# Two more products with the identity turned into DMA transposes, in an attention and mixer kernel on one core

## The chip, the cores and the metric

The kernel runs on one core of one Trainium2 chip, as one program. Its time is the device time of one execution in microseconds (us); of several executions the median is taken. Lines such as L384 are line numbers of the kernel before.

The core's engines run their own instruction queues side by side: TensorE (PE in the profile) does matmuls and writes PSUM; VectorE (DVE) and ScalarE (ACT) work element by element; GpSimd (POOL) here mostly issues loads that convert float32 to float16; SyncE (SP) issues stores and DMA transposes. All DMAs are carried out by 16 DMA engines.

## The reference

There are 8 batches, 8 heads, 576 tokens, 16 beacon tokens and a head size of 64. First comes attention, causal over the tokens, with the beacons visible to all; then a mixer over the 512 channels of the 8 heads.

```python
k_all = np.concatenate([beacon_k, k], axis=2)
v_all = np.concatenate([beacon_v, v], axis=2)
scores = np.matmul(q, k_all.transpose(0, 1, 3, 2)) / np.sqrt(D)    # causal over the tokens
a = softmax(scores)
x = np.matmul(a, v_all)                                            # as (batch, token, channel)
h = x.transpose(0, 2, 1) @ U @ V                                   # low rank (32) over the tokens
u = x + h.transpose(0, 2, 1)
out = u + np.maximum(u @ w_ch1, 0.0) @ w_ch2                       # 512 -> 2048 -> 512
```

## The kernel before

**Attention.** The heads are taken in pairs: pair `p` is batch `p // 4`, heads `2 * (p % 4)` and the next. For each pair the kernel needs q and k with the head size on the partitions (`qT`, `kT`), the scores (`score_units`, L329, the exponential on ACT in L335, the mask on DVE in L305 and L307), and the product with v (`av_unit`, L357). Its result, divided by the sum, goes to `xb` (L366), which holds x of one batch with tokens on the partitions.

For batches 0 to 3, q and k are turned on TensorE: the loads land in a staging tile, DVE copies a pair of heads into a packed tile `pr` (`regroup`, L252, and L254 for the beacons' rows of k), TensorE transposes it (L259), and DVE copies the result to `qT` and `kT` (L292, L297). For batches 4 to 7 (`DT0 = 4`), ten DMA transposes per batch do that from SP's queue (`turns`, L607). They are issued five at a time, in the order k0, q0, k1, q1, k2, then q2, k3, q3, k4, q4.

**Mixer.** `uT` holds u of all batches with the channels on the partitions. `mix_units` makes it for one batch: `head` (L393) is the product with U, `most` the product with V for the first 496 tokens (L417), `end` that for the last 80 (L429). Where `turned` is false, x itself is added inside the same PSUM banks by products with the identity (`x_into`, L372), and DVE and ACT copy the sum out (L406, L408). Where `turned` is true, `turn` has SP issue five DMA transposes of `xb` into `uT` (L384), and DVE adds the product to what they wrote (L404). Before the change, batch 0 has a version of its own (`first_mix`), batches 1 and 2 add x on TensorE, and batches 3 to 7 use the DMA transposes.

The two large products work on nine blocks of 512 rows of u, from `mlp_units`: 16 units `g_unit` (w_ch1, L487, with the ReLU on ACT in L500 or on DVE in L502), then four row tiles of four units `c_unit` each (w_ch2, L512). At the end u itself is added. For blocks 1 to 8, four DMA transposes (L481) have brought a piece of `uT` back to rows (`ut`), and DVE adds it while it copies the result out of PSUM (L525). For block 0, `turned` is false: four products with the identity add u in PSUM (L520), and DVE (L529) and ACT (L527) copy the result out in turns. Then SP stores it (L530).

**Order.** The order of the instructions of PE, ACT, DVE, SP and POOL is written out by hand. The units of the mixer stand in a list `queue`. After each step of a pair, `fill` takes some of them and puts them behind it, so that TensorE has large products to do while the pair's small steps wait for DVE and ACT. `feed` appends the units of a block as soon as its rows are known. `mix(b)` sets `head`, `most` and `end` of batch b into the list: `n` units stand ahead of `head`, `k` between `head` and `most`, three between `most` and `end`. In the loop over the pairs from batch 2 on, the step of pair 12 (batch 3, first pair) issues five of the fifth batch's ten transposes and then calls `mix(2)`; the step of pair 13 issues the other five. Scores of pair `p + 1` are computed at the start of the step of pair `p`, so the fifth batch's `qT` and `kT` are first read at the start of the step of pair 15.

Nothing reorders SP's queue: an instruction that waits holds up everything behind it. The same is true of DVE's.

Of the kernel before, what the change touches and what calls it, by code (L numbers as in the profile page):

```python
# [18 lines left out]
P = 128  # L19
# [11 lines left out]
def kernel(  # L31
# [14 lines left out]
    B, H, S, D = q.shape  # L46
# [6 lines left out]
    NH2 = H // 2  # L53
# [48 lines left out]
    def pst(shape, dtype, name):  # L102
        return psum.tile(shape, dtype, tag="ps", name=name)
# [364 lines left out]

        return head, begin, rest

    def mlp_units(t0, n, dst, flip, turned=True, last=False):


        units = []
        gT = {}
        held = {}

        def turn():
            ut = utp.tile([P, 4, DM], F16, name="ut", tag="ut")
            for cc in range(NCC):  # L480
                nc.sync.dma_start_transpose(out=ut[:, :, ts(cc, P)], in_=uT[:, cc, ds(t0, 4 * P)])  # L481
            gT["u"] = ut

        def g_part(dc, upto):
            g, done = held.get(dc) or (pst([P, 512], F32, name="gps"), 0)
            for cc in range(done, upto):
                nc.tensor.matmul(  # L487
                    g[:, 0:n], w1[:, cc, ts(dc, P)], uT[:, cc, ds(t0, n)], start=(cc == 0), stop=(cc == NCC - 1)
                )
            held[dc] = g, upto  # L490

        def g_unit(dc):
            if dc == 0:
                gT["t"] = gtp.tile([P, NDC, 512], F16, name="gT", tag="gT")
                if turned:
                    turn()
            g_part(dc, NCC)
            g, _ = held.pop(dc)
            if (dc % 3 if not turned else (dc + flip) % 2 or dc in (5, 6, 7)):
                nc.scalar.activation(out=gT["t"][:, dc, 0:n], in_=g[:, 0:n], func=AF.Relu)  # L500
            else:
                nc.vector.tensor_scalar_max(out=gT["t"][:, dc, 0:n], in0=g[:, 0:n], scalar1=0.0)  # L502

        cps = {}

        def c_unit(i, part):
            m = min(P, n - P * i)
            if part == 0:
                cps["t"] = pst([P, DM], F32, name="cps")
            ps = cps["t"]  # L510
            for dc in range(4 * part, 4 * part + 4):
                nc.tensor.matmul(  # L512
                    ps[:m, :], gT["t"][:, dc, ds(P * i, m)], w2[:, dc, :], start=(dc == 0),
                    stop=turned and dc == NDC - 1, skip_group_check=True,
                )
            if part == 3:
                ob = outp.tile([P, DM], F32, name="ob", tag="ob")
                if not turned:
                    for cc in range(NCC):
                        nc.tensor.matmul(  # L520
                            ps[:m, ts(cc, P)], uT[:, cc, ds(t0 + P * i, m)], ident, start=False, stop=True,
                            skip_group_check=True,
                        )
                if turned:
                    nc.vector.tensor_tensor(out=ob[:m, :], in0=ps[:m, :], in1=gT["u"][:m, i, :], op=ALU.add)  # L525
                elif i % 2:
                    nc.scalar.activation(out=ob[:m, :], in_=ps[:m, :], func=AF.Copy)  # L527
                else:
                    nc.vector.tensor_copy(out=ob[:m, :], in_=ps[:m, :])  # L529
                nc.sync.dma_start(out=dst(i, m), in_=ob[:m, :])  # L530

        def c_half(i, part):
            hs = ds(DM // 2 * (part // 2), DM // 2)
            if part % 2 == 0:
                cps["t"] = pst([P, DM // 2], F32, name="cph")
            for dc in range(NDC // 2 * (part % 2), NDC // 2 * (part % 2 + 1)):
                nc.tensor.matmul(  # L537
                    cps["t"], gT["t"][:, dc, ts(i, P)], w2[:, dc, hs], start=(dc == 0), stop=(dc == NDC - 1)
                )
            if part % 2:  # L540
                ob = outp.tile([P, DM // 2], F32, name="oh", tag="ob")
                nc.vector.tensor_tensor(out=ob, in0=cps["t"], in1=gT["u"][:, i, hs], op=ALU.add)
                nc.sync.dma_start(out=dst(i, P)[:, hs], in_=ob)

        units += [lambda dc=dc: g_unit(dc) for dc in range(NDC)]
        for i in range((n + P - 1) // P):
            c = c_half if last and i == n // P - 1 else c_unit
            units += [lambda i=i, part=part, c=c: c(i, part) for part in range(4)]
        return units, g_part
# [24 lines left out]
    rows = out.rearrange("b s c -> (b s) c")  # L574
    NP = B * NH2
    NBLK = B * S // 512
    Ls, qTs, xbs = {}, {}, {}

    def load_batch(b):
        if b < DT0:  # L580
            Ls[b] = qk_tiles()
            emit_loads(b, Ls[b], vss[b % 2])
        else:
            v_loads(v[b], beacon_v[b], vss[b % 2])
# [70 lines left out]
    def qkT_of(p):  # L655
        b, c = divmod(p, NH2)
        new_qT_of(p)
        copies = [(act_copy, nc.vector.tensor_copy) if p == 0 else (nc.vector.tensor_copy,)] * 2
        turns = by_heads(Ls[b][0], c)
        for i, t in enumerate(prs.get(p, ())):  # L660
            if t is not None:
                turns[i] = in_pair(prs[p])[i]
        if p == 0:
            turns[0] = beacons_apart(turns[0], Ls[0][0][0], 0)
        return qkT_units(turns, qTs[b], kTs[b % 2], c, copies)

    def scores_of(p):
        b, c = divmod(p, NH2)
        return score_units(c, qTs[b], kTs[b % 2], [expts[(2 * p + i) % NE] for i in range(2)], p < NM)
# [10 lines left out]
    NF = 2  # L680
# [3 lines left out]
    DT0 = 4  # L684
    LAG = 10
# [7 lines left out]
    queue = []  # L693
    state = {"t": 0}

    def fill_turns(tr, n):
        for u in tr[:n]:
            u()
        del tr[:n]
# [8 lines left out]
    def feed(b):  # L708

        while state["t"] < NBLK and 512 * (state["t"] + 1) <= S * (b + 1):  # L710
            t = state["t"]
            units, state["part"] = mlp_units(
                512 * t, 512, lambda i, m, t=t: rows[ds(512 * t + P * i, m), :], t % 2, t > 0, t == NBLK - 1
            )
            queue.extend(units)
            state["t"] += 1

    def mix(b):

        turned = b >= NF and len(queue) >= LAG + 7  # L720
        turn, head, parts = mix_units(xbs[b], S * b, turned)
        if turned:
            turn()
        n = (LAG + 3 * (b == B - 1)) if turned else 2 if b >= NF else 0
        k = 2 if turned else 1
        most, end = parts
        rest = queue[n + k + 3 :]
        queue[:] = queue[0:n] + [head] + queue[n : n + k] + [most] + queue[n + k : n + k + 3] + [end]
        for _ in range(4):
            queue.extend(rest[:1] + [None])  # L730
            del rest[:1]
        queue.extend(rest)
        feed(b)

    with tc.manual_schedule(engines={ENG.PE, ENG.Activation, ENG.DVE, ENG.SP, ENG.Pool}):
# [11 lines left out]
        t0, sc = qkT_of(0), scores_of(0)  # L747
# [66 lines left out]
        t0, sc = qkT_of(4), scores_of(4)  # L814
# [14 lines left out]
        for p in range(NH2, NP1):  # L829
            b, c = divmod(p, NH2)  # L830
# [31 lines left out]
        t0, sc, t1 = qkT_of(NP1), scores_of(NP1), qkT_of(NP1 + 1)  # L862
# [5 lines left out]
        for p in range(NP1, NP):  # L868
            b, c = divmod(p, NH2)
            if c == 0 and b + 1 < B:  # L870
                load_batch(b + 1)
            if c == (2 if b + 2 == DT0 else 1) and DT0 <= b + 2 < B:
                load_whole(b + 2)
            if c == 0 and b + 1 == DT0:
                tr = turns(b + 1)
            if c == NH2 - 1 and DT0 < b + 2 < B:
                tr = turns(b + 2)
            sc = scores_of(p + 1) if p + 1 < NP else []
            qk = qkT_of(p + 2) if p + 2 < min(NP, DT0 * NH2) else []
            av = av_of(p)  # L880
            if c == NH2 - 1 or c == 0 and b + 1 == DT0:
                fill_turns(tr, NT)
            if c == 0 and b > NF:
                mix(b - 1)
            if c == (1 if b + 1 == DT0 else 0):
                fill_turns(tr, NT)
            seq = sc[0:1] + av[0:1] + qk[0:1] + sc[1:3] + qk[1:2] + av[1:2]
            if p + 3 < min(NP, DT0 * NH2):
                seq.append(lambda p=p: regroup_of(p + 3))
            quota = QUOTA.get(b, 9)  # L890
            done = 0
            for i, u in enumerate(seq):
                u()
                want = quota * (i + 1) // len(seq)
                fill(want - done)
                done = want
        mix(B - 1)
        guard()

# [53 lines left out]
    with tc.If(n_bad != 0, label="general"):  # L953
        with tc.For_i(0, B, 1) as bi:
# [14 lines left out]
            for t0 in range(0, S, 512):  # L969
                n = min(512, S - t0)  # L970
# [32 lines left out]
```

## Time and profile before

| | |
|---|---|
| median of 3 runs | 356.88 us (356.86 to 357.33) |
| the profiled execution | 356.95 us, of which the profile's span is 355.3 us |
| granted TensorE clock | 1.00 of full speed |
| TensorE busy | 348.2 us, 98% of the span |
| VectorE, ScalarE, GpSimd busy | 187.3, 167.4 and 97.5 us |
| DMA from GpSimd's queue | 87440 packets, 18.18 MB |
| DMA from the hardware queues (SP, ACT) | 56464 packets, 22.25 MB |
| products with the identity in block 0 (L520) | 16 |
| products with the identity in `mix_units` and `first_mix` (L372) | 60 |
| DMA transposes L481, L384, L607 | 32, 25, 40 |

The busy time of an engine is the time in which one of its instructions ran. A matmul's recorded time includes its way through the array, so two that follow each other overlap in the records: what a matmul costs TensorE is read from the distance between starts. An idle time in the timeline stands in brackets behind the instruction that ended it, with what released it. All times in the views are microseconds from the start of the span.

### The profile page before, as it was taken

The numbers are of one execution on the slowest core, as the hardware profiler recorded it, in microseconds if no ns is written. First come the engines' busy times: TensorE is split into PE (matmuls) and PEld (weight loads), VectorE is DVE, ScalarE is ACT, GpSimd is POOL, SyncE is SP. The second block draws the span as 40 slices with busy tenths as digits, with TensorE's granted clock in tenths as the row PEclk, the third lists the DMA queues.
The fourth block names the chain that finished last, engine by engine and source line by source line (L and its number), as shares of the span: only waits on it lengthen the run. The fifth ranks groups of instructions, "written<-read, shape, count | busy, mean of one in ns | idle before, by whom it ended". The sixth has DMA issues, their size and how long they took to land.

```text
span 355.3 us, 7823 instructions
## 1 busy us (share of the span) xinstructions
PE 348.2 (98%) x3130; PEld 174.2 (49%) x3130; DVE 187.3 (53%) x482; ACT 167.4 (47%) x361; POOL 97.5 (27%) x137
## 2 busy tenths in 40 slices
PE   8999999999999999999999999999999999999995
PEld 3665555455554444444444444444454444444443
DVE  5656965588975543754455457345746522313311
ACT  5967841587654563466444664566503202301400
POOL 8956704427437048206800500000000000000000
PEclk9999999999999999999999999999999999999999
DMA  9999999999999979999999993142014413013111
GB/s 181 100 203 169 159 199 171 226 155 123 107 95 149 180 104 131 147 192 104 142 136 178 135 130 81 61 105 52 31 61 102 56 59 105 15 59 100 21 58 67
DMA packets 144170, 41.28 MB, mean 116 GB/s; under 512 B 129024, under 2 KB 139616, under 8 KB 144128
## 3 DMA queue, kind: packets, MB, share of 16 engines
q0 software_dynamic: 87440, 18.18, 66.5%
q1 hardware_dynamic: 56464, 22.25, 33.2%
q8 instruction: 26, 0.43, 0.5%
q10 hardware_dynamic: 224, 0.30, 0.3%
q14 instruction: 16, 0.13, 0.1%
HBM read 37.37 MB, written 9.44 MB: 132 GB/s over the span
## 4 chain that ended last, share of the span: by engine, by line
PE 89%; DMA 3%; DVE 2%; ACT 2%; SPq 1%; issue 0%; ACTq 0%
PE gps L487 34%; PE cps L512 32%; PE po L357 8%; PE sps L329 7%; DMA uT<-xb 2%; ACT expt L335 2%; SPq L384 1%; PE tps L259 1%; DMA stk<-in_k_dram 1%; PE cph L537 1%; PE tps L265 1%; PE ups L372 1%; PE qtp L393 1%; PE sps L321 1%; PE ups L417 1%; DVE uT L404 1%
## 5 line engine op out<-in xcount | busy, mean ns | idle before, releaser
L335 ACT ACTIVATE expt<-sps 128x496 f16<-128x496 f32 (+2 forms) x256 | 111.1, 542 | 57.6 <-PE sps L329 57.5
L487 PE MATMUL gps<-uT,w 128*128 128x512 f16 x576 | 135.7, 379 | 0.1
L512 PE MATMUL cps<-w,gT 128*128 128x512 f16 x560 | 132.7, 380 | 0.0
L500 ACT ACTIVATE gT<-gps 128x512 f16<-128x512 f32 x86 | 51.8, 607 | 94.1 <-PE gps L487 92.3
L487 PEld LDWEIGHTS <-w 128*128 128x128 f16 x576 | 51.9, 98 | 59.5 <-issue 3.8
L512 PEld LDWEIGHTS <-gT 128*128 128x128 f16 x560 | 49.9, 98 | 59.2 <-issue 6.9
L502 DVE TENSOR_SCALAR gT<-gps 128x512 f16<-128x512 f32 x58 | 40.0, 690 | 47.5 <-PE gps L487 46.7
L525 DVE TENSOR_TENSOR ob<-cps,ut 128x512 f32<-128x512 f32 x31 | 21.4, 690 | 49.6 <-PE cps L512 46.7
L207 POOL DMA_DIRECT2D vs<-in_v_dram x50 | 39.6, 809 | 21.4 <-DMA st<-in_k_dram 5.6
L357 PEld LDWEIGHTS <-expt 128*128 128x128 f16 (+1 forms) x960 | 36.2, 98 | 15.1 <-issue 2.6
L357 PE MATMUL po<-vs,expt 128*128 128x65 f16 (+1 forms) x960 | 39.4, 194 | 0.4 <-DVE expt L305 0.3
L329 PE MATMUL sps<-qT,kT 64*128 64x80 f16 (+4 forms) x384 | 34.3, 282 | 0.6 <-DVE uT L404 0.4
L366 DVE TENSOR_TENSOR xb<-po,rec 128x320 f16<-128x320 f32 x64 | 31.5, 492 | 2.2
L305 DVE TENSOR_TENSOR expt<-expt,bigmask 128x512 f16<-128x512 f16 x54 | 22.6, 419 | 11.7 <-ACT expt L335 11.7
L365 DVE RECIPROCAL rec<-po 128x5 f32<-128x5 f32 x64 | 12.0, 187 | 23.9 <-PE po L357 23.9
L329 PEld LDWEIGHTS <-kT 64*128 64x128 f16 x384 | 11.9, 94 | 22.3 <-issue 13.7
L189 POOL DMA_DIRECT2D vs<-in_beacon_v_dram x8 | 4.3, 543 | 61.4 <-PE po L357 61.4
L595 POOL DMA_DIRECT2D st<-in_q_dram x20 | 16.9, 865 | 3.3 <-DMA vs<-in_v_dram 2.2
L595 POOL DMA_DIRECT2D st<-in_k_dram x20 | 16.9, 874 | 0.9 <-DMA vs<-in_v_dram 0.9
L404 DVE TENSOR_TENSOR uT<-ups,uT 128x496 f16<-128x496 f32 x20 | 12.1, 668 | 7.5 <-PE cps L512 3.9
L292 DVE COPY qT<-tps 128x576 f16<-128x576 f16 (+1 forms) x16 | 11.8, 735 | 3.2 <-PE tps L265 2.2
L292 DVE COPY kT<-tps 128x576 f16<-128x576 f16 (+1 forms) x16 | 11.7, 734 | 2.3 <-PE tps L265 1.5
(92 smaller groups left out, 147.2 us busy)
## 6 DMA issues: line engine op xcount, KB each, us to landing
out_dram<-ob SPq DMA_DIRECT2D x35, 256.0 KB, 2.1
vs<-in_v_dram POOLq DMA_DIRECT2D x18, 128.0 KB, 7.7
w<-in_moe_w_ch_dram POOLq DMA_DIRECT2D x4, 512.0 KB, 6.1
w<-in_moe_w_ch_dram POOLq DMA_DIRECT2D x2, 1024.0 KB, 11.6
st<-in_k_dram POOLq DMA_DIRECT2D x12, 128.0 KB, 6.7
st<-in_q_dram POOLq DMA_DIRECT2D x12, 128.0 KB, 9.8
st<-in_k_dram POOLq DMA_DIRECT2D x2, 576.0 KB, 13.1
st<-in_q_dram POOLq DMA_DIRECT2D x2, 576.0 KB, 16.0
```

Of the source, the lines that this page charges most:

```text
L207: nc.gpsimd.dma_start(out=dst[a : a + nq[j], j, :, :], in_=src[hs, ds(q0[j], nq[j]), :].rearrange("h p d -> p h d"))
L292: copy(out=whole[:, :, ds(w * a, w)], in_=ps[:, 0 : TP * w].rearrange("x (j p) -> x p j", j=w),)
L305: nc.vector.tensor_tensor(out=e4, in0=e4, in1=bigmask, op=ALU.min)
L329: nc.tensor.matmul(ps[g, i][:, ds(o, w)], kT[hp, c, ds(P * ch, P)], qT[hp, c, ds(qa, w)], start=not early, stop=True, skip_group_check=early,)
L335: nc.scalar.activation(out=ex[i][:, ds(SLOT * g, gw[g])], in_=ps[g, i][:, 0 : gw[g]], func=AF.Exp, scale=scale)
L357: nc.tensor.matmul(po[:, j, :], ex[0 : nk[c], ds(blk[(c, j)], P)], vs[0 : nk[c], ds(c * H * E + h * E, E)], start=(c == 0), stop=(c == j),)
L366: nc.vector.tensor_tensor(out=xb[:, :, ds(h * D, D)], in0=po[:, :, 0:D], in1=r.broadcast_to([P, NT, D]), op=ALU.mult)
L487: nc.tensor.matmul(g[:, 0:n], w1[:, cc, ts(dc, P)], uT[:, cc, ds(t0, n)], start=(cc == 0), stop=(cc == NCC - 1))
L500: nc.scalar.activation(out=gT["t"][:, dc, 0:n], in_=g[:, 0:n], func=AF.Relu)
L502: nc.vector.tensor_scalar_max(out=gT["t"][:, dc, 0:n], in0=g[:, 0:n], scalar1=0.0)
L512: nc.tensor.matmul(ps[:m, :], gT["t"][:, dc, ds(P * i, m)], w2[:, dc, :], start=(dc == 0), stop=turned and dc == NDC - 1, skip_group_check ...
L595: nc.gpsimd.dma_start(out=dst[a : m[j], j, :, :], in_=src[:, ds(q0[j], nq[j]), :].rearrange("h p d -> p h d"))
```

## The change

Block 0 of the mixer is made with `turned=True`: its u comes back to rows by four DMA transposes on SP's queue (L481), and DVE adds it in all four row tiles (L525). The four products with the identity in each row tile go. The ReLUs of block 0 stay divided between ACT and DVE as they were, by a new argument `early`.

`mix(b)` takes the DMA transposes for every batch from `NF = 2` on; before, it also asked for at least 17 units in the list, which batch 2 did not have. `n`, the number of units ahead of `head`, becomes `min(LAG, len(queue) - 8)` for it. In the program's order that is 8 units in place of 2, and 2 in place of 1 between `head` and `most`.

In the step of pair 12, `mix(2)` now comes ahead of the first five of the fifth batch's transposes, so that SP issues the five of batch 2's x first.

```diff
-    def mlp_units(t0, n, dst, flip, turned=True, last=False):
+    def mlp_units(t0, n, dst, flip, turned=True, last=False, early=False):
...
-            if (dc % 3 if not turned else (dc + flip) % 2 or dc in (5, 6, 7)):
+            if (dc % 3 if early else (dc + flip) % 2 or dc in (5, 6, 7)):
                 nc.scalar.activation(out=gT["t"][:, dc, 0:n], in_=g[:, 0:n], func=AF.Relu)
...
             units, state["part"] = mlp_units(
-                512 * t, 512, lambda i, m, t=t: rows[ds(512 * t + P * i, m), :], t % 2, t > 0, t == NBLK - 1
+                512 * t, 512, lambda i, m, t=t: rows[ds(512 * t + P * i, m), :], t % 2, True, t == NBLK - 1, t == 0
             )
...
     def mix(b):
 
-        turned = b >= NF and len(queue) >= LAG + 7
+        turned = b >= NF
         turn, head, parts = mix_units(xbs[b], S * b, turned)
         if turned:
             turn()
-        n = (LAG + 3 * (b == B - 1)) if turned else 2 if b >= NF else 0
+        n = 0 if not turned else LAG + 3 if b == B - 1 else min(LAG, len(queue) - 8)
...
-            if c == NH2 - 1 or c == 0 and b + 1 == DT0:
+            if c == NH2 - 1:
                 fill_turns(tr, NT)
             if c == 0 and b > NF:
                 mix(b - 1)
-            if c == (1 if b + 1 == DT0 else 0):
+            if c == 0 or c == 1 and b + 1 == DT0:
                 fill_turns(tr, NT)
```

## The prediction

> **What bounds the kernel now.** I read the page first, then TensorE's timeline, then the chain of waits and VectorE's and SP's timelines where the change touches them. The page's busy times:
>
> ```profile
> PE 348.2 (98%) x3130; PEld 174.2 (49%) x3130; DVE 187.3 (53%) x482; ACT 167.4 (47%) x361; POOL 97.5 (27%) x137
> DMA  9999999999999979999999993142014413013111
> ```
>
> TensorE is the bound in all but the first slices, so a product taken out is time gained, unless TensorE then waits for something else. The DMA engines are busy without a break through the first half, where both new groups of transposes lie. TensorE's timeline (start, length, line, tiles, count):
>
> ```profile
> 55.95 0.39 PE L520 MATMUL cps<-ident,uT 128*128 128x128 f16 x4
> 56.18 0.31 PE L372 MATMUL uend<-ident,xb 80*128 80x80 f16 x4
> ...
> 98.82 1.05 PE L372 MATMUL ups<-ident,xb 112*128 112x112 f16 x16
> 99.80 0.39 PE L417 MATMUL ups<-Vsb,qts 32*128 32x496 f16 x4
> ...
> 103.46 0.31 PE L372 MATMUL uend<-ident,xb 80*128 80x80 f16 x4
> 103.60 0.31 PE L429 MATMUL uend<-Vend,qts 128*128 128x80 f16 x4
> ...
> 120.55 0.58 PE L329 MATMUL sps<-qT,kT 64*128 64x496 f16 x4
> ```
>
> Distances between starts price the products; the last row is the first use of the fifth batch's `qT` and `kT`. VectorE's timeline where the third batch's q and k arrive:
>
> ```profile
> 59.56 0.19 DVE L254 COPY pr<-st 16x128 f16<-16x128 f16 x1 [1.83 <-DMA st<-in_beacon_k_dram]
> 59.78 0.90 DVE L252 COPY pr<-st 96x768 f16<-96x768 f16 x2
> 60.70 0.19 DVE L254 COPY pr<-st 16x128 f16<-16x128 f16 x1
> 60.90 0.57 DVE L252 COPY pr<-st 96x768 f16<-96x768 f16 x1
> 61.47 0.76 DVE L292 COPY qT<-tps 128x576 f16<-128x576 f16 x1
> 62.60 0.76 DVE L292 COPY kT<-tps 128x576 f16<-128x576 f16 x1 [0.37 <-PE tps L259]
> ```
>
> VectorE waits 1.83 us for the beacons' rows of k, issued at 39.31 and landed 20.2 us later, and has only 0.37 us to spare until `kT`. The chain of waits goes on from there to the scores:
>
> ```profile
> 62.60 0.76 DVE kT L292
> 63.35 0.09 DVE kT L297
> 63.44 0.05 issue
> 63.49 0.58 PE sps L329 x4
> ```
>
> So the kernel is on the edge of a load here, though TensorE looks full. SP's timeline around the fifth batch's transposes:
>
> ```profile
> 91.36 1.22 SPq L607 DMA_TRANSPOSE kT<-st  x1
> 102.87 0.35 SPq L530 DMA_DIRECT2D out_dram<-ob  x1
> ...
> 108.98 1.25 SPq L607 DMA_TRANSPOSE qT<-st  x1
> ```
>
> The last of the ten, which the scores at 120.55 need, is issued at 108.98 and lands 6.8 us later, at 115.8: 4.8 us to spare.
>
> **Taken from TensorE.** L520: four products shift the next start by 56.18 - 55.95 = 0.23; four row tiles, 0.92 us. The third batch's L372: 99.80 - 98.82 = 0.98 and 103.60 - 103.46 = 0.14. Together 2.04 us, of which 0.46 lies ahead of the scores at 63.49 and 1.58 behind it.
>
> **Added to VectorE and taken from ScalarE.** Two of block 0's row tiles move from ACT (L527, 0.60 each) to DVE (L525, 0.69 each, 0.61 from start to start); two settlings of the third batch's u move likewise (L408, 0.58, to L404, 0.67). Three of these four lie in slack: VectorE idles 1.16, 1.48 and 3.10 us between 104 and 117, and 0.5 near 71. The second row tile's addition does not: in the changed order it stands between the last `pr` copy and the `qT` copy, and adds 0.61 us to the chain shown.
>
> **Four transposes for block 0.** ACT and DVE finish the first batch's u between 23 and 26.3 us, and SP is idle there, so the four are issued at about 23 to 28.5. They are needed at 56 by L525, so their own landing (7.5 us at most in L481's rows) does not matter. What they take from the loads does. Each moves 131 KB, 0.52 MB in all. From 25 to 29 us the loads alone move 204 GB/s; from 20 to 24, when SP's small copies run beside them, both together move 208. A byte of one displaces a byte of the other: 0.52 MB / 0.205 = 2.6 us. Upper end 3.5 (at 107 to 113 us some 1400 small packets of transposes and stores cost the loads about 0.36 MB at 150 GB/s, 0.87 us per 512-packet transpose). Lower end 0: from 71 to 74 three issued transposes moved nothing while the loads ran on, so they could live on gaps. But the beacons' rows stand behind 20 us of loads and the transposes will not wait that long; and the only gap I find is about 0.5 us near 37. I take a delay D of 2.0 us.
>
> Nearly all of D reaches the scores. `pr` is done at 61.47 + D; then 0.61 (new addition), 0.67 (`qT`), 0.67 + 0.16 (`kT`) and 0.05: 63.63 + D in place of 63.49. What TensorE saved ahead of that point is lost in the wait. With the 1.58 us saved behind it, the balance is 0.14 + D - 1.58 = D - 1.44: +0.56 us for D = 2.0, between -1.44 and +2.06. Other loads have more room: `w1`'s last quarter lands at 41.3 and is used at 44.26, the first half of `w2` lands at 47.6 and is used at 51.18. A stall at one of them would only take from the one at 63.49, not add to it.
>
> The Trainium skill (Advanced Engine Details and Errata, X-Bar Transpose) says that transposing DMAs are as fast as ordinary ones, 350 to 400 GB/s. By that an estimate of D is 1.4 us and the balance zero; the late transposes here peak near 300 GB/s, and the loads they would displace run at 205.
>
> **Five transposes for the third batch.** xb is complete at 94.65. `most` now comes some 12.8 us into the step that starts at 94.08 (ten `c_unit`s of 0.865, three L357 groups of 0.47, and the small steps), about 106.9. The fourth of the five is issued near 99 and lands 5 to 7 us later. No wait there; at worst 0.6 us, the TensorE idle time near 182 when the same happened to a later batch. `head`, moved behind six more units, costs nothing: the same products are issued.
>
> **What they push back on SP.** The fifth batch's first five were issued from 84.57 to 92.6, before x was complete; now they stand behind x. From 94.7: five L384 at 1.51 (7.57 for five at 130.14), five L607 at 1.30, two stores at 0.4, four L607 at 1.40: the last is issued at about 115.2 instead of 108.98. GpSimd's next k and q loads (104.75 to 113.1, landing until about 118) run beside it. With the 6.8 us of before it lands at 122.0; with an idle DMA (2.4 us, the late L481) at 117.6. TensorE wants it at 120.55 less the 1.12 saved in between: 119.4. The wait is 0 to 2.6 us; with loads ending before it does I take 1.3. SP's later work does not suffer: it waits 7.48 us for stores after 110.32.
>
> **Sum.** -1.44 + 2.0 + 1.3 = +1.86 us on the profiled 356.95 is 358.8; the median stood 0.07 lower, so 358.7.
>
> **Rivals.** *The DMA engines have room* (faster): the new transposes live on gaps and the turned q lands within 4.3 us. Place: the waits at 63 and 119. For it: 71 to 74, above, and DMA pauses at 101 to 103. Against: no pause from 25 to 59. Then -1.44: 355.5. It decides where D stays under 0.7 and the last landing under 4.3 us. *Only the load is late*: 356.95 + 0.56 = 357.5. For it: SP issued L607 at 1.30 and landings of 3.7 at 103; against: 6.3 to 6.8 for the last three before. *Only the turned q is late*: 355.5 + 1.3 = 356.8. For it: transposes served in gaps early on; against: the equal sums of 20 to 24 and 25 to 29. *Both at their upper ends*: 355.5 + 3.5 + 2.6 = 361.6; the two waits share nothing, but each is at its worst only if the transposes are as dear as at 107.
>
> The Trainium skill (DMA: Bandwidth & Descriptors, Issuing engines are not separate DMA queues) holds that DMAs from different engines use the same 16 and interleave. By that the first rival falls; the row of 20 to 24 agrees, that of 71 to 74 does not.
>
> **Chances.** Both waits as forecast 0.52, time 357.7 to 360.5; only the load 0.16; only the turned q 0.12; room on the DMA engines 0.15; both at their worst 0.05. About 0.2% (0.7 us) is what a measurement here can tell from no change. Faster: the room case and the low side of the turned-q case, 0.19. Same: most of the one-sided cases, 0.19. Slower 0.62. The range from 355.4 to 360.6 takes in the room case and the bulk of the forecast.
>
> **What would show it.** L520 gone, L372 at 40, L481 at 36, L384 at 30. VectorE's wait at L254 for the beacons grows from 1.83 to about 3.8 us, and the third batch's first scores start near 65.6 instead of 63.49. At the fifth batch's first scores, near 121 in the new time, TensorE waits for a DMA into `qT`. If L254's wait stays near 1.8, D is wrong; if no wait stands at those scores, the second step is. A wait of L404 on `uT<-xb` would be one that I ruled out.

## The result and the profile after

The changed kernel takes 362.58 us (median of 6, 360.61 to 363.32) against 357.20 us (median of 6, 356.86 to 357.39): a ratio of 1.0144, 95% interval 1.0117 to 1.0170. It is slower by 5.4 us between the medians, where 1.8 was forecast. The profiled execution took 361.55 us, with a span of 359.9; the working below is on it, and the median lies 1.0 us above it. Its two executions with a granted clock of 1.00 took 361.55 and 360.61 us, the four with 0.995 took 362.40 to 363.32; what lowered the clock is not shown.

From the page of the changed kernel, the engines' busy times:

```profile
PE 346.6 (96%) x3094; PEld 172.4 (48%) x3094; DVE 188.6 (52%) x486; ACT 165.4 (46%) x357; POOL 97.6 (27%) x137
```

TensorE is busy 1.6 us less than before, as products went, while the span grew by 4.6: what it gained and more became waiting. The three places are in TensorE's timeline of the changed kernel (start, length, line, tiles, count; in brackets the idle time and what ended it):

```profile
29.38 1.04 PE L487 MATMUL gps<-uT,w 128*128 128x512 f16 x4 [0.52 <-DMA w<-in_moe_w_ch_dram]
...
39.63 1.04 PE L487 MATMUL gps<-uT,w 128*128 128x512 f16 x4 [1.65 <-DMA w<-in_moe_w_ch_dram]
40.60 0.58 PE L329 MATMUL sps<-qT,kT 64*128 64x496 f16 x4
...
66.13 0.58 PE L329 MATMUL sps<-qT,kT 64*128 64x496 f16 x4 [0.90 <-DVE kT L297]
...
109.36 0.39 PE L417 MATMUL ups<-Vsb,qts 32*128 32x496 f16 x4
109.69 0.39 PE L329 MATMUL sps<-qT,kT 64*128 64x336 f16 x6
110.28 0.25 PE L329 MATMUL sps<-qT,kT 64*128 64x208 f16 x1 [0.21 <-DVE qT L292]
110.86 0.25 PE L329 MATMUL sps<-qT,kT 64*128 64x208 f16 x1 [0.33 <-DVE uT L404]
111.04 2.76 PE L512 MATMUL cps<-w,gT 128*128 128x512 f16 x12
...
124.04 0.39 PE L329 MATMUL sps<-qT,kT 64*128 64x496 f16 x2 [1.28 <-DMA qT<-st]
126.52 0.37 PE L329 MATMUL sps<-qT,kT 64*128 64x464 f16 x2 [2.10 <-DMA qT<-st]
```

The same scores in the kernel before, those at 40.60 and the group at 109.69:

```profile
38.41 0.58 PE L329 MATMUL sps<-qT,kT 64*128 64x496 f16 x4
...
106.90 0.48 PE L329 MATMUL sps<-qT,kT 64*128 64x336 f16 x8
107.31 1.04 PE L512 MATMUL cps<-w,gT 128*128 128x512 f16 x4
```

The third batch's first scores start at 66.13 in place of 63.49. Most of that delay is paid long before them, at 29.38 and 39.63, for two pieces of `w1`: counted from pair 3's first scores (16.70, and 17.02 before), the scores at 40.60 are 2.51 us late and those at 66.13 are 2.96 us late. In between 0.46 us of products went, and the 0.90 us at 66.13 came. The waits near 110 are new. At 124 and 126.5 the fifth batch's first scores wait 3.38 us for its turned q.

VectorE's timeline of the changed kernel at the first and the second place, and then the chain of waits at the first (start, length, what):

```profile
62.18 0.19 DVE L254 COPY pr<-st 16x128 f16<-16x128 f16 x1 [2.49 <-DMA st<-in_beacon_k_dram]
...
110.14 2.40 DVE L404 TENSOR_TENSOR uT<-ups,uT 128x496 f16<-128x496 f32 x4
```

```profile
43.12 19.04 DMA st<-in_beacon_k_dram
...
64.08 0.59 DVE ob L525
64.67 0.67 DVE qT L292
65.34 0.67 DVE kT L292
66.00 0.08 DVE kT L297
66.09 0.05 issue
66.13 0.58 PE sps L329 x4
```

The beacons' rows arrive at 62.16 and no longer at about 59.5. They were under way for 19.0 us in place of 20.2; what made them late is that GpSimd issued them at 43.12 in place of 39.31. Behind them stands block 0's second addition, L525, with 0.59 us.

SP's timeline of the changed kernel at the third place:

```profile
97.02 7.52 SPq L384 DMA_TRANSPOSE uT<-xb  x5
104.71 1.19 SPq L607 DMA_TRANSPOSE kT<-st  x1
...
111.35 1.89 SPq L530 DMA_DIRECT2D out_dram<-ob  x2
113.33 1.34 SPq L607 DMA_TRANSPOSE qT<-st  x1
...
117.60 1.99 SPq L607 DMA_TRANSPOSE kT<-st  x1
119.68 1.20 SPq L607 DMA_TRANSPOSE qT<-st  x1
```

The last of the ten goes out at 119.68 and lands 6.7 us later.

The distances between the first scores of chosen pairs, after minus before, say where the 4.6 us of span come from. The forecast's terms stand beside them.

| stretch | from starts at (before; after) | measured | forecast |
|---|---|---|---|
| start to pair 3 | 17.02; 16.70 | -0.32 | 0 |
| to pair 8, third batch's first scores | 63.49; 66.13 | +2.96 | 0.14 + 2.0 |
| to pair 13 | 94.08; 96.42 | -0.30 | -0.46 |
| to pair 17 | 130.38; 136.14 | +3.42 | -1.12 + 1.3 |
| to pair 23 | 182.83; 188.59 | 0 | 0 |
| to pair 24 | 190.45; 195.08 | -1.13 | 0 |
| to the end | 355.3; 359.9 | -0.03 | 0 |

Two rows are far from the forecast: +3.42 for +0.18, and a gain of 1.13 us near 190 where nothing was changed. The first theory was that three losses are separate: loads displaced by block 0's transposes, settlings of the third batch's u (the instructions that take u out of PSUM into `uT`, here L404) that hold PSUM banks, and the fifth batch's q turned late. The rivals were those of the prediction, that only one of them counts, and that SP's queue is simply too full.

### The profile page after: what moved, and what is told of

It is laid out like the page before. It is cut to its first block, busy times and chain, and to the rows that moved or that the text cites. A ratio compares the mean times of both kernels' runs of the same rounds, so it can differ in the third digit from the quotient of the medians.

```text
span 359.9 us, 7769 instructions
## 1 busy us (share of the span) xinstructions
PE 346.6 (96%) x3094; PEld 172.4 (48%) x3094; DVE 188.6 (52%) x486; ACT 165.4 (46%) x357; POOL 97.6 (27%) x137
## 4 chain that ended last, share of the span: by engine, by line
PE 74%; DMA 15%; POOL 6%; issue 2%; DVE 2%; SPq 1%; POOLq 0%
PE gps L487 30%; PE cps L512 29%; PE po L357 6%; PE sps L329 6%; DMA st<-in_beacon_k_dram 5%; DMA st<-in_k_dram 4%; DMA vs<-in_v_dram 3%; POOL vs L207 2%; DMA qT<-st 2%; POOL st L192 1%; SPq L607 1%; PE cph L537 1%; PE tps L259 1%; PE qtp L393 1%; DVE pr L252 1%
## 5 line engine op out<-in xcount | busy, mean ns | idle before, releaser
L525 DVE TENSOR_TENSOR ob<-cps,ut 128x512 f32<-128x512 f32 x35 | 24.1, 689 | 50.3 <-PE cps L512 48.2
L366 DVE TENSOR_TENSOR xb<-po,rec 128x320 f16<-128x320 f32 x64 | 31.4, 491 | 2.2
L404 DVE TENSOR_TENSOR uT<-ups,uT 128x496 f16<-128x496 f32 x24 | 14.5, 665 | 6.4 <-PE ups L417 3.6
```

The source lines that it names most:

```text
L366: nc.vector.tensor_tensor(out=xb[:, :, ds(h * D, D)], in0=po[:, :, 0:D], in1=r.broadcast_to([P, NT, D]), op=ALU.mult)
```

## The experiments

Differences of a place in the kernel are counted below from each run's own start of pair 3's first scores, since these scores start between 16.70 and 18.74 us. Medians and ratios are against the kernel before on the same chip.

### Block 0's u alone

```diff
-    ... t % 2, t > 0, t == NBLK - 1
+    ... t % 2, True, t == NBLK - 1, t == 0
```

The argument `early` goes with it, as in the change.

> Only block 0's u is turned by DMA; the third batch's x and SP's later order stay as in the kernel before. Theory (the four transposes take DMA time from a queue of loads that has no pause): VectorE's wait at L254 for the beacons' rows ends near 62.2 instead of 59.56, the third batch's first scores start near 66.1 instead of 63.49, 0.46 us of the saved products comes back behind that point: about +2.2 us on the kernel before, 359.2. Rival 1 (VectorE's addition in place of ScalarE's copy is what makes the scores late, the loads are not touched): scores at 63.6, and the kernel ends 0.3 us earlier than before, 356.7. At the fifth batch's first scores neither expects a wait for a DMA.

358.42 us (ratio 1.0049, 1.0018 to 1.0079). VectorE's wait for the beacons' rows was 2.24 us and the third batch's first scores started 2.76 us later; no wait for a DMA stood at the fifth batch's scores. The displaced load is there without the other part. The time is lower than expected by 0.8 us, because the gain near 190 came here too.

### Third batch's x alone, in the new SP order and in the old

First with all of the change to `mix` and to `fill_turns`, then without the latter, so that five of the fifth batch's transposes go ahead of x again:

```diff
-        turned = b >= NF and len(queue) >= LAG + 7
+        turned = b >= NF
...
-        n = (LAG + 3 * (b == B - 1)) if turned else 2 if b >= NF else 0
+        n = 0 if not turned else LAG + 3 if b == B - 1 else min(LAG, len(queue) - 8)
```

> Only the third batch's x is turned by DMA, with the changed order on SP; block 0 is made as before. Theory: scores at 63.49 as before; 1.12 us of products saved; the four settlings on VectorE cost up to 0.9 us near 110; at the fifth batch's first scores TensorE waits about 3.4 us for the last turned q: about +2.4 to +3.2 us on the kernel before, 359.3 to 360.1. Rival 1 (the early part makes the whole loss): -1.1 us or better, 355.8.

> As the run with x alone, but SP issues the fifth batch's first five transposes ahead of the third batch's x, as in the kernel before. The same nine transposes run, only their order differs. Theory (SP's order pushes the last five back): SP issues the last q near 109 as before, it lands some 4 us ahead of its use, and no DMA wait stands at the fifth batch's first scores: between -0.6 and +0.4 us on the kernel before, 356.3 to 357.3. Rival 2 (five more transposes slow the DMA engines down whatever their order): the last q lands late all the same, a wait of 2 to 3 us stays, 359 to 360.

With the new order 359.03 us (1.0049, 1.0028 to 1.0070), 0.3 us under the lower end of what was expected; with the old one 356.09 us (0.9967, 0.9954 to 0.9979), faster than the kernel before and 0.2 us under the lower end. Both hold the gain near 190, which the expectations left out. From TensorE's timeline with the new order, where the waits near 108 are 0.20 and 0.34 us, the late q:

```profile
123.30 0.37 PE L329 MATMUL sps<-qT,kT 64*128 64x464 f16 x2 [1.96 <-DMA qT<-st]
```

and with the old order:

```profile
108.40 0.25 PE L329 MATMUL sps<-qT,kT 64*128 64x208 f16 x1 [0.21 <-DVE qT L292]
108.98 0.25 PE L329 MATMUL sps<-qT,kT 64*128 64x208 f16 x1 [0.34 <-DVE uT L404]
...
120.82 0.58 PE L329 MATMUL sps<-qT,kT 64*128 64x496 f16 x4
```

The late q is a matter of the order alone: the last of the ten transposes is issued at 111.46 with the old order and at 116.71 with the new. The wait for it is 1.96 us here, where about 3.4 was expected after the 3.38 of the changed kernel. The waits at 108 do not care about the order. The forecast's own term for them was nothing; in the changed kernel, from start to start, the second group of scores takes 1.35 us to the next product (109.69 to 111.04) in place of 0.41 (106.90 to 107.31), so they cost 0.94.

### Idle transposes: four, eight, and four late

The kernel before keeps its products L520; `turn` is called more often, and what the extra calls bring back is never read.

```diff
+                for _ in range(idle):
+                    turn()
                 if turned:
                     turn()
```

`idle` is 1 for block 0 in the first, 2 for block 0 in the second, and 1 for block 7 in the third.

> The kernel before, with four more DMA transposes of block 0's u into a tile that nobody reads, at the place where the change issues them. No product is saved and no work moves to VectorE. Theory: the beacons' rows land 2.6 us later and the scores start near 65.9 (2.6 later less what VectorE had to spare): about +2.3 us on the kernel before, 359.3, and TensorE waits for w1's quarters before that as in the changed kernel. Rival 1 (VectorE's addition): no change, 357.0.

> The kernel before with eight DMA transposes of block 0's u (1.05 MB) whose result is never read, in place of four. Theory (a byte of a transpose displaces a byte of the loads): the delay of the third batch's first scores doubles from the 3.0 us of four to about 5.2 to 6.0, so they start near 69, and the time is 362.2 to 363.2. Rival (a fixed price, such as one transfer that straggles and holds GpSimd's queue up once, whatever the bytes): about as with four, 3.0 to 3.5 us, 360.3 to 360.8.

> The kernel before with four idle DMA transposes of the u of block 7 (0.52 MB), late in the kernel, where the loads are done. Theory (the price of block 0's transposes is the loads that they displace): nothing, 356.9 to 357.6. Rival (the price lies in issuing them on SP's queue, in the tile they are written to or in the stores behind them): TensorE waits 1 to 3 us more in that stretch, 358.2 to 360.3.

Four: 360.31 us (1.0086, 1.0064 to 1.0107). Eight: 363.23 us (1.0166, 1.0141 to 1.0192). Four late: 357.19 us (0.9993, 0.9971 to 1.0015). The third batch's first scores come 2.77, 6.19 and -0.02 us later than before. With four, the median lies 1.0 us above the 359.3 expected and the profiled execution, 359.48, near it; with eight, the 6.19 is a little above the 6.0 expected at most. VectorE's line for the beacons' rows with four, with eight, and with four late:

```profile
63.15 0.19 DVE L254 COPY pr<-st 16x128 f16<-16x128 f16 x1 [3.02 <-DMA st<-in_beacon_k_dram]
```

```profile
66.34 0.19 DVE L254 COPY pr<-st 16x128 f16<-16x128 f16 x1 [3.54 <-DMA st<-in_beacon_k_dram]
```

```profile
59.97 0.19 DVE L254 COPY pr<-st 16x128 f16<-16x128 f16 x1 [1.90 <-DMA st<-in_beacon_k_dram]
```

The loss needs neither VectorE's additions nor the missing products, grows with the bytes, by somewhat more than they do, and is not there late in the kernel, where the loads are done. With four, 2.01 of the 2.77 us, and with eight, 4.94 of the 6.19, stand already at the scores of pair 7 (43.75 before, 46.01 and 48.70), behind waits for `vs` and `w1`; so L254's wait alone grows little, and the start of the scores is what counts. So the first rival of the prediction, that there is room, falls, and so does a fixed price.

### The change with the old SP order

```diff
-            if c == NH2 - 1:
+            if c == NH2 - 1 or c == 0 and b + 1 == DT0:
...
-            if c == 0 or c == 1 and b + 1 == DT0:
+            if c == (1 if b + 1 == DT0 else 0):
```

> The changed kernel with SP's order of before: the fifth batch's first five transposes ahead of the five of the third batch's x. Theory (three losses that do not share a resource: the loads displaced by block 0's transposes, the settlings of the third batch's u that hold PSUM banks, the fifth batch's q turned late): VectorE still waits about 2.5 us for the beacons' rows of k, and the third batch's first scores still start near 66.1 to 66.5; the wait of 3.4 us for a DMA into qT at the fifth batch's first scores is gone. By the profiled ends of the two parts alone (+2.7 up to the step of pair 23 with block 0's u alone, +0.3 with x alone and this order, less the 1.1 that both gain after it): +1.9 us, 359.0, between 358.3 and 359.7. Rival (SP's queue as a whole is too full, whatever its order): a DMA wait of over 1 us stays at those scores, and the time stays over 360.5.

357.97 us (1.0022, 1.0007 to 1.0037), 0.3 us under the lower end of what was expected. The third batch's first scores came 2.58 us late and the waits of 0.21 and 0.34 us were there, at 111.94 and 112.52. At the fifth batch's first scores TensorE's timeline shows no wait (this execution started 1.7 us late); one of 0.39 us for a turned q stands at 193.94, at the seventh batch's:

```profile
122.54 1.89 PE L487 MATMUL gps<-uT,w 128*128 128x512 f16 x8
124.36 0.58 PE L329 MATMUL sps<-qT,kT 64*128 64x496 f16 x4
```

The two parts alone multiply to 1.0049 x 0.9967 = 1.0016, and together they measured 1.0022. That is no clean test, because each part alone holds the gain near 190, about 1.2 us or 0.35%, and it can come only once. Counted once, the parts give 1.005 here, a little more than was measured, and 1.013 with the new order (1.0049 x 1.0049 and 0.35%), inside the interval of the change. So the times show no sign that one part makes the other dearer. Most of the 1.4% was the order on SP (1.0144 to 1.0022, from separate comparisons); the rival, that SP's queue is too full whatever its order, falls.

### Where the settlings stand, and in how many pieces

Two attempts to win back the 0.94 us in the faster version, third batch's x alone with the old order. The first puts `most` behind the scores of its step, with `n = 9` and `k = 3` for batch 2. The second cuts it:

```diff
-        at = [most] + at
+        at = [lambda: most((0, 1))] + at[:1] + [lambda: most((2, 3))] + at[1:]
```

> Third batch's x alone with SP's order of before (the one that ran 1.1 us under the kernel before), and most placed behind the scores of its step in place of between their two groups (nine units ahead of head, three between head and most). Theory (the two waits of 0.21 and 0.34 us at the settlings, with the starts they delay some 0.9 us, come from PSUM banks that the four settlings hold while VectorE does one after the other, just when the next scores ask for banks): the waits go or shrink, and the time is 355.2 to 355.7. Rival (the settlings' time on VectorE has to be waited for wherever they stand): waits of the same sum at another line, 355.9 to 356.4.

> Third batch's x alone, SP's order of before, with the third batch's most split into two halves of two PSUM banks, a unit of the mixer between them. Theory (four settlings in one go keep VectorE 2.4 us and four banks; whatever stands behind them, scores or the copy of kT, waits): the waits of 0.21 and 0.34 us at the scores near 108 go and none of over 0.3 us takes their place at kT near 113; 0.5 to 0.9 us under the 356.1 of the unsplit one: 355.2 to 355.6. Rival (VectorE has no room for them between 104 and 117 however they are cut): 355.9 to 356.4.

Behind the scores: 356.06 us (0.9960, 0.9942 to 0.9979), like the version that it was made from, as the rival had it; the waits at 108 went, and one of 0.84 us came at 114.27, where the scores waited for a copy of `kT` that stood behind the four settlings on VectorE. Cut in two: 356.75 us (0.9992, 0.9972 to 1.0011), above both ranges expected. It is no gain, and probably a loss against the uncut 0.9967 (0.9954 to 0.9979), though the two intervals just overlap. There the waits did go and none took their place, as the theory had it: at pair 16 the kernel was 1.33 us ahead of the uncut one, 0.87 of it a unit of the mixer that a longer list puts off, and 0.46 gained. It was given back at 183 us, as TensorE's timeline of the cut version shows:

```profile
181.69 0.38 PE L329 MATMUL sps<-qT,kT 64*128 64x496 f16 x2
182.23 0.35 PE L329 MATMUL sps<-qT,kT 64*128 64x464 f16 x1 [0.16 <-DVE uT L404]
182.81 0.35 PE L329 MATMUL sps<-qT,kT 64*128 64x464 f16 x1 [0.23 <-DVE uT L404]
183.39 1.02 PE L512 MATMUL cps<-w,gT 128*128 128x512 f16 x4 [0.23 <-DVE uT L404]
184.91 0.62 PE L357 MATMUL po<-vs,expt 128*128 128x65 f16 x15 [0.49 <-DVE xb L366]
```

And VectorE's line for what they wait for, in the same run:

```profile
180.92 2.42 DVE L404 TENSOR_TENSOR uT<-ups,uT 128x496 f16<-128x496 f32 x4 [3.44 <-DMA uT<-xb]
```

The fifth batch's settlings start when its x lands, at 180.9, whatever TensorE has gained; TensorE asks for the banks at 181.69, and from start to start (1.70 us for the scores where 0.52 is usual, 1.52 for the unit behind them where 0.87 is) it loses 1.83 us.

### The wait that the kernel before has at 183

The same place explains the gain of 1.13 us in the table. TensorE's timeline of the kernel before:

```profile
182.83 0.38 PE L329 MATMUL sps<-qT,kT 64*128 64x496 f16 x2
183.41 0.35 PE L329 MATMUL sps<-qT,kT 64*128 64x464 f16 x1 [0.20 <-DVE uT L404]
183.99 0.35 PE L329 MATMUL sps<-qT,kT 64*128 64x464 f16 x1 [0.23 <-DVE uT L404]
184.28 1.04 PE L512 MATMUL cps<-w,gT 128*128 128x512 f16 x4
185.47 0.61 PE L357 MATMUL po<-vs,expt 128*128 128x65 f16 x15 [0.16 <-DVE ob L525]
```

By starts (1.45 for 0.52, 1.19 for 0.87) it loses 1.25 us here. The settlings begin 1.31 us ahead of those scores, at 181.52 (the profile puts VectorE's wait before them down to a product of TensorE, not to the landing of x, so that the landing holds them here is inferred); in the changed kernel, in both parts alone and in x with the old order they begin 2.4 to 2.7 us ahead, and the loss is absent. An experiment took the kernel before and cut only the fifth batch's `most` in two, the second half behind the scores and a unit:

```diff
+        if b == DT0:
+            at = queue[n + k : n + k + 5]
+            mid = [lambda: most((0, 1))] + at[:4] + [lambda: most((2, 3))] + at[4:]
```

> The kernel before, with most of the fifth batch (no part of the change) split into two halves of two PSUM banks, the second behind the next scores and a unit. Theory (the kernel before itself loses about 1.25 us near 183 us, because the fifth batch's x lands late, at 181.5, and four late settlings on VectorE hold four PSUM banks when the next scores ask for four; the changed kernel and both parts alone are free of it because the landing falls 1.1 to 1.4 us earlier there): the waits of 0.20, 0.23 and 0.16 at that place go, and the time is 0.8 to 1.3 us under the kernel before, 356.0 to 356.5. Rival (that 1.25 us is the records of one execution, or comes back at the next wait for a landing): 356.9 to 357.4.

> As the one before, and the fifth batch's most split too. Theory (with x alone the fifth batch's x already lands in time, so there is no second loss to take away): no further gain, within 0.4 us of the one before. Rival (the two losses are separate and both are there): a further 0.8 to 1.2 us, 354.2 to 354.6.

The kernel before with this cut: 357.05 us (0.9993, 0.9980 to 1.0005), no difference that can be told. The waits at the scores went, but 0.27 us appeared behind them, `<-DVE xb L366`, and by starts only about 0.5 of the 1.25 us was saved; the time is the rival's. With both cuts in the version with x alone: 356.68 us (0.9977, 0.9965 to 0.9989), no gain over the one cut that can be told. The time is the theory's by luck, since its reason, that there is no second loss to take away, does not hold: the one cut had run into the loss at 183. By starts, the second cut won about 0.9 us of it back by the scores of pair 24, and most of that was lost again right there, where a turned q of the seventh batch was late by 0.50 us at 189.65.

So the place of the loss in the kernel before is shown, and that it is absent wherever the settlings begin 2.4 us or more ahead of the scores. It is not shown why they begin relatively earlier once either part is in: measured back from those scores, the five transposes are issued at the same point within 0.6 us (167.57 before, 167.28 with x in the old order). That stays open.

## Why the prediction was wrong in size

**The side was right, and so were the two places named, but the first loss began earlier.** "VectorE's wait at L254 for the beacons grows from 1.83 to about 3.8 us, and the third batch's first scores start near 65.6" measured 2.49 and 66.13; the wait for a DMA into `qT` stood at the fifth batch's first scores.

**The delay D of 2.0 us was too small.** From the forecast's own bytes over the observed rate, 2.6, it was cut to 2.0 for gaps that the transposes might live on. The runs show 2.58 to 2.96 at the scores for four, and 6.19 for eight. The uncut quotient was the better estimate, and still low; the row from 71 to 74 that spoke for gaps misled. The Trainium skill (DMA: Bandwidth & Descriptors, Issuing engines are not separate DMA queues), which the forecast cited, says that DMAs from different engines use the same 16 and interleave. The traces agree: 207 GB/s with the loads alone from 24 to 28 us, 206 and 200 with the four transposes beside them. The sentence that other loads have room was wrong too: two pieces of `w1` cost 0.52 and 1.65 us of waiting, and the scores at 40.60 were already 2.51 us late; only the last quarter of `w1` and the first half of `w2` had been read. As the forecast said, this came out of the same 2.96 and was not added to it, and so L254's wait grew to 2.49 and not to 3.8. The 0.61 us of L525 in the chain measured 0.59.

In the Trainium skill (DMA: Bandwidth & Descriptors, Latency and other measured facts) a transposing DMA moves 261 GB/s in one measured kernel, with a non-contiguous middle dimension, and an estimate from that is 0.52 / 0.261 = 2.0 us for four. No delay measured here is that short: 0.52 MB cost 2.6 to 3.0 us, and 1.05 MB cost 6.19.

**"Three of these four lie in slack" missed a step.** The forecast counted VectorE's idle time between 104 and 117 in sum, and found room for the two settlings added there. It left out what four settlings in a row, 2.40 us where before ACT and VectorE shared them, hold meanwhile: four PSUM banks, just when the next scores ask for four. This cost 0.94 us, a term at zero in the sum. That x itself lands in time was right.

**The turned q was forecast to wait 1.3 us, 2.6 at most, and waited 3.38.** The last transpose was to be issued at 115.2; less the 2.34 us by which the kernel was late there, it went at 117.3. The five transposes of x and the first five behind them went as forecast. Two stores took 1.98 us of SP in place of 0.8, and the four transposes ahead of the last took 6.35 in place of 5.6. With the landing at 6.7 us, near the forecast's long end, the wait passed the end of its range. It is the largest term that was mis-sized: from the eight products at 120.87 to the four at 126.83 TensorE lost 3.63 us by starts (5.96 for 2.33) where 1.3 was forecast. With the 0.94 of the settlings that makes 3.63 - 1.3 + 0.94 = 3.27, which accounts for the 3.24 us by which the stretch to pair 17 missed the forecast. Why the wait was 1.96 us with the third batch's x alone is not settled; there the last transpose was issued 22.2 us behind pair 13's first scores, here 23.3.

**A loss of the kernel before was not in the sum.** The idle time near 182 was named in the prediction, as a price that x might have to pay again, and not as 1.25 us that could go. In the sum 1.86 + 0.82 (to pair 8) + 0.16 + 3.24 - 1.13 - 0.35 (start and end) = 4.6.

**The rivals.** "Only the load" and "only the turned q" are both refuted as an account of the whole; each exists alone, and with the gain near 190 counted once the two add up to the whole within its interval. "Both at their upper ends" gave 361.6 and the profiled execution took 361.55, but that is luck: the first loss stayed under its end, the second passed it, and neither the 0.94 us of the settlings nor the 1.13 us gained near 190 was in it. "The DMA engines have room" is refuted at the start, and true late in the kernel, at no cost.

## What to carry to other kernels

Before a product is traded for a DMA, read where the loads stand at the moment when that DMA would run: while they are the bound, the new bytes are taken from them, and here 0.92 us of products bought 2.6 to 3.0 us of waiting. On a queue that issues in order, place each transfer by the deadline of those behind it: the same five transposes made the kernel 0.5% slower ahead of the fifth batch's and 0.3% faster behind them. And where a kernel has a row of such deadlines, time gained at one of them has to be followed to the next: in the profiles of two kernels that removed their waits at 108 the gain was given back at 114 or at 183.

The version worth keeping is the third batch's x alone with the order of before, 356.09 us; block 0's u is better left on TensorE.

## What the runs showed of the hardware beyond that

Transposes and loads that run together did not raise the rate. DMA rates by stretch, first of the kernel before, then of the changed one with four transposes on their way (stretch, its length in us, granted clock, time that packets took as a share of 16 engines' time, GB/s):

```profile
24.00:26.00 2.00, 1.00 1.26 207
26.00:28.00 2.00, 1.00 1.31 207
28.00:30.00 2.00, 1.00 1.66 176
```

```profile
24.00:26.00 2.00, 1.00 1.26 206
26.00:28.00 2.00, 1.00 1.30 200
28.00:30.00 2.00, 1.00 1.48 115
```

From 28 to 30 the rate even fell, to 115 GB/s, while GpSimd waited 2.57 us for a piece of `w1` before it issued its next load. That is where part of the difference between 2.6 us and the 2.96 measured may come from; it is read from one execution. The four transposes themselves took 8.6 to 9.2 us to land there, where L481 took 7.5 at most in the kernel before.
